# Turning the first batches' q and k with plain products in an attention and two-MLP kernel

## The chip, the cores and the metric

The kernel runs on one core of a Trainium2 chip. The metric is device time in microseconds (us) of one execution. Three timed runs of the kernel before gave 852.64, 853.40 and 854.97 us; the median is 853.4 us.

## The reference

Batched attention with a narrow causal mask feeds a SwiGLU layer and then a SoLU layer with a norm. All inputs are float32 or, for the weights, float64 words.

```python
def attn(q, k, v):                       # each 4 x 8 x 576 x 64
    scores = q @ k.T / sqrt(64)
    # heads 0-3: the 32 last keys; heads 4-7: every 4th of the 128 last keys
    scores = where(mask, scores, -1e9)
    return softmax(scores) @ v

x = attn(q, k, v).transpose(0, 2, 1, 3).reshape(2304, 512)
x = (silu(x @ w_gate) * (x @ w_val)) @ w_out         # 512 -> 1536 -> 512
h = x @ w_in                                         # 512 -> 1024
s = h * softmax(h)
out = ((s - mean(s)) / sqrt(var(s) + 1e-6) * g_ln) @ w_out2
```

## The kernel before

**Stages.** The 2304 tokens are cut into 12 blocks of 192. Per block, stage A is the gate and value products (line 1458), B the product with w_out (line 1542); per 128 tokens, C is the product with w_in (line 1590) and D the last one (line 1718). These run on TensorE (PE) as three float16 passes each, since every operand is split into a high and a low float16 part. The weights come as float64 words in 1 MB loads (line 667); VectorE (DVE), ScalarE (ACT) and GpSimd (POOL) turn the words into float32 and split them (lines 690 to 870), one half slab after the other.

**Attention of batches 0 and 1.** These two batches (FIRST = 2) work in float32 and in pairs of heads, four pairs a batch. `load_qk` brings q or k of a pair into one tile: head 0 on partitions 0 to 47, head 1 on partitions 64 to 111, twelve rows of 64 numbers on each partition. `prep_T` then turns the tile on TensorE: twelve steps, in each one 48x64 piece of each head against a 48x48 identity, the piece being the loaded weights and the identity what streams. Head 0's piece goes through TensorE's transpose form (line 1130, one instruction), head 1's is an ordinary float32 product (line 1132, which the chip runs as two instructions, called passes below). Both heads write one PSUM bank pair, head 0 on PSUM partitions 0 to 63, head 1 on 64 to 127. ACT or DVE copies the result out (lines 1145, 1148). With q and k, four pairs and two batches there are 16 turned tiles, 192 steps. Behind them `g1` makes scores (lines 1306 and 1313), `g2` turns the probabilities (line 1358) and `g3` multiplies by v (line 1392). Batches 2 and 3 turn q and k by DMA and are not touched.

**What sets the order.** Nothing is left to a scheduler on the chip. At build time every piece of work is a step with an engine, a cost and its dependences; the class `Plan` plays the engines through with these costs and takes, of the steps that are ready first, the one with the lowest number in the table `PRI` (2190 numbers). The instructions stand in each engine's queue in that order. Where the plan finds TensorE idle before its 320th us, it puts in products of `ones` with itself (line 379, 128 columns each, "fills" below). The plan's cost of one turned tile is 12 x `ttc` = 12 x 0.09 = 1.08 us at full clock; `ttc` is the same before and after. SP issues nearly all loads in the plan's order, and a load waits in that queue for its buffer.

Of the kernel before, what the change touches and what calls it, by code (L numbers as in the profile page):

```python
# [334 lines left out]
def kernel(  # L335
# [13 lines left out]
    nc = tc.nc  # L349
# [173 lines left out]
    def dve(n):  # L523
        return n / 960 + 0.065
# [4 lines left out]
    def act(n):  # L529
        return n / 1200 + 0.09  # L530
# [1524 lines left out]
```

## Time and profile before

| | before |
|---|---|
| timed runs, median (range) | 853.4 us (852.64 to 854.97) |
| the profiled execution, its own time | 854.95 us |
| its span, first to last instruction | 852.8 us |
| PE busy | 838.3 us (98%) |
| DVE, ACT, POOL busy | 492.2 (58%), 438.0 (51%), 214.6 us (25%) |
| mean granted TensorE clock | 0.928 of full speed |

Busy is the time in which an engine had an instruction in hand; for PE it is no measure of how fast that work went. The granted clock is 1.0 at 2.4 GHz and 0.5 at 1.2 GHz. The profiled execution took 2.15 us more than its span and 1.55 us more than the median of the runs.

### The profile page before, as it was taken

What the parts mean: (1) busy time and instruction counts of PE and PEld (TensorE: products, weight loads), DVE (VectorE), ACT (ScalarE), POOL (GpSimd) and SP (SyncE); (2) the same over time, 40 slices, a digit from 0 to 9 for tenths busy, and PEclk for the clock granted to TensorE, in tenths of its full rate; (3) what the DMA queues carried; (4) which work ended last, traced back from release to release, by engine and by line L of the source; (5) the groups of instructions that cost most, each with busy time, mean ns of one, the idle gap of its engine ahead of it and who ended that gap; (6) DMA issues with size and microseconds to landing.
All of it is one profiled execution on the core that took longest, in us unless ns stands there. A gap on an engine that the chain in (4) does not pass through costs nothing.

```text
span 852.8 us, 21072 instructions
## 1 busy us (share of the span) xinstructions
PE 838.3 (98%) x8965; PEld 686.7 (81%) x8965; DVE 492.2 (58%) x1082; ACT 438.0 (51%) x825; POOL 214.6 (25%) x190
## 2 busy tenths in 40 slices
PE   9999999999999999999999999999999999999997
PEld 8777887978998897886778659888987789888753
DVE  1331852924988885976676777747738433132472
ACT  1123742843764366786877645666564443262432
POOL 2110410313265543222421423333432000020000
PEclk7665985966999999999999999999999999999999
DMA  9922234432413736114486254443311112001101
GB/s 226 280 96 69 69 116 126 136 103 73 128 51 91 184 115 144 51 40 92 86 161 121 60 95 106 86 90 80 69 37 33 32 29 42 14 1 26 39 0 50
DMA packets 132605, 73.46 MB, mean 86 GB/s; under 512 B 115104, under 2 KB 117280, under 8 KB 132000
## 3 DMA queue, kind: packets, MB, share of 16 engines
q1 hardware_dynamic: 132512, 72.12, 35.3%
q8 instruction: 70, 1.15, 0.6%
q14 instruction: 23, 0.19, 0.1%
HBM read 47.71 MB, written 4.72 MB: 61 GB/s over the span
## 4 chain that ended last, share of the span: by engine, by line
PE 91%; DVE 4%; SPq 2%; DMA 1%; ACT 1%; issue 1%; POOL 0%; ACTq 0%; POOLq 0%
PE ps L1458 33%; PE ps L1542 14%; PE ps L1590 10%; PE ps L1718 10%; PE ps L1132 7%; PE ps L1130 4%; PE ps L379 4%; PE ps L1392 2%; PE ps L1313 1%; PE ps L1199 1%; PE ps L967 1%; SPq L929 1%; PE ps L1265 1%; DMA vbig<-in_v_dram 1%; DVE area L603 1%
## 5 line engine op out<-in xcount | busy, mean ns | idle before, releaser
L1458 PE MATMUL ps<-x,gv 128*128 128x192 f16 x3456 | 307.7, 251 | 1.3 <-ACT ps L575 0.8
L1458 PEld LDWEIGHTS <-gv 128*128 128x128 f16 x3456 | 295.2, 100 | 9.8 <-issue 1.4
L1542 PE MATMUL ps<-uhl,area 128*128 128x192 f16 x1728 | 151.6, 247 | 1.5 <-DVE yhl L603 1.3
L1542 PEld LDWEIGHTS <-area 128*128 128x128 f16 x1728 | 143.3, 98 | 6.3 <-issue 2.0
L1590 PE MATMUL ps<-area,yhl 128*128 128x512 f16 x432 | 98.6, 379 | 0.0
L1718 PE MATMUL ps<-area 128*128 128x512 f16 x408 | 94.2, 379 | 0.8 <-DVE yhl L603 0.8
L1590 PEld LDWEIGHTS <-yhl 128*128 128x128 f16 x432 | 41.0, 98 | 44.6
L1470 ACT ACTIVATE si<-ps,c_gv 128x384 f32<-128x384 f32 x72 | 41.5, 578 | 64.1 <-PE ps L1458 63.4
L1479 DVE SCALAR_TENSOR_TENSOR u<-ps,c_gv,si 128x384 f32<-128x384 f32 x60 | 36.5, 610 | 63.4 <-ACT si L1470 63.4
L1718 PEld LDWEIGHTS <-area 128*128 128x128 f16 x408 | 38.9, 98 | 42.3 <-issue 1.1
L683 POOL TENSOR_TENSOR area<-area 128x512 int32<-128x512 int32 x28 | 40.6, 1466 | 78.9 <-DVE wsc L791 33.8
L1650 POOL TENSOR_TENSOR sml<-sml,nhalf 128x2 f32<-128x2 f32 x18 | 14.6, 809 | 156.1 <-DVE sml L1647 151.6
L1132 PE MATMUL ps<-ident,qk 48*64 48x48 f32 x264 | 51.1, 284 | 0.0
L1229 POOL TENSOR_TENSOR se<-se,sml 96x768 f32<-96x768 f32 x16 | 24.1, 1509 | 94.7 <-ACT si L1485 60.4
L1485 ACT ACTIVATE si<-u 128x384 f32<-128x384 f32 x60 | 31.1, 518 | 25.7 <-DVE u L1479 25.7
L1216 ACT ACTIVATE se<-se,sml 96x128 f32<-96x128 f32 x96 | 37.2, 388 | 7.2 <-DVE sml L1510 3.6
L1132 PEld LDWEIGHTS ps<-ident,qk 48*64 48x64 f32 x264 | 31.9, 170 | 9.6
L379 PE MATMUL ps<-ones 128*128 128x128 bf16 x462 | 37.0, 250 | 2.2 <-POOL kT L1095 1.5
L615 POOL TENSOR_TENSOR uhl<-u,uhl 128x768 f16<-128x768 f32 x12 | 19.7, 1668 | 75.5 <-ACT uhl L598 75.5
L379 PEld LDWEIGHTS <-ones 128*128 128x128 bf16 x462 | 33.8, 115 | 3.5 <-POOL kT L1095 1.5
L615 POOL TENSOR_TENSOR qk<-qk,qk 96x768 f16<-96x768 f32 x16 | 26.7, 1667 | 36.2 <-DVE qk L594 14.1
L1130 PE MATMUL ps<-ident,qk 48*64 48x48 f32 x132 | 34.1, 259 | 0.0
(249 smaller groups left out, 1235.2 us busy)
## 6 DMA issues: line engine op xcount, KB each, us to landing
area<-in_moe_w_out_dram SPq DMA_DIRECT2D x10, 1024.0 KB, 5.0
area<-in_moe_w_gate_dram SPq DMA_DIRECT2D x6, 1024.0 KB, 7.3
area<-in_moe_w_val_dram SPq DMA_DIRECT2D x6, 1024.0 KB, 8.5
area<-in_moe_w_in_dram SPq DMA_DIRECT2D x4, 1024.0 KB, 5.0
qk<-in_v_dram SPq DMA_DIRECT2D x9, 384.0 KB, 4.0
qk<-in_q_dram SPq DMA_DIRECT2D x20, 144.0 KB, 3.2
qk<-in_k_dram SPq DMA_DIRECT2D x18, 144.0 KB, 3.3
out_dram<-area SPq DMA_DIRECT2D x10, 256.0 KB, 2.0
```

What stands on the lines that cost most here:

```text
L379: nc.tensor.matmul(out=ps_t[4][:, 0, 256:384], lhsT=ones, rhs=ones, start=True, stop=True)
L615: step("POOL", n / 480 + 0.05, lambda: nc.gpsimd.tensor_tensor(out=lo(), in0=src(), in1=hi(), op=ALU.subtract), r=list(sk) + list(hk), w=lk)
L683: step("POOL", 1.27, lambda: nc.gpsimd.tensor_tensor(out=ti[:, x], in0=ti[:, x], in1=part[:, x], op=ALU.add), r=rk, w=tk)
L1130: nc.tensor.transpose(out=o, in_=i, identity=ident[rows, rows])
L1132: nc.tensor.matmul(out=o, lhsT=i, rhs=ident[rows, rows], start=True, stop=True)
L1216: nc.scalar.activation(out=smv[:, n], in_=smv[:, n], func=ACTF.Exp, bias=nm[:, n:n + 1], scale=1.0, accum_out=su[:, n:n + 1])
L1458: nc.tensor.matmul(out=cut(view()[:, ff, w]), lhsT=wt[:, a, kk, (f % 4) * 128:(f % 4) * 128 + 128], rhs=tokens(x[:, c, kk]), start=(w == 0 ...
L1470: step("ACT", act(384) + 0.06, lambda: nc.scalar.activation(out=si, in_=view()[:, :, 0], func=ACTF.Silu, scale=c_gv[:, b, 2 * ci:2 * ci + 1]),
L1479: nc.vector.scalar_tensor_tensor(out=uu, in0=view()[:, :, 1], scalar=c_gv[:, b, 2 * ci + 1:2 * ci + 2], in1=si, op0=ALU.mult, op1=ALU.mult)
L1542: nc.tensor.matmul(out=bk.get()[:, 0, cc * BLK:cc * BLK + BLK], lhsT=whl[6 + f // 4][:, a, f % 4, c * 128:(c + 1) * 128], rhs=uhl[:, e, f] ...
L1590: nc.tensor.matmul(out=bk.get()[:, half], lhsT=yhl[:, i, c, o:o + 128], rhs=w_in_hl[m][:, e, c % 2, half * 512:half * 512 + 512], start=(c ...
L1718: nc.tensor.matmul(out=bk.get()[:, 0], lhsT=zt[:, c, kk], rhs=whl[11 + half][:, e, kk % 4], start=(kk == 0 and n == 0), stop=(kk == 7 and ...
```

## The change

In `prep_T` both heads' pieces are ordinary products with the identity; the branch with the transpose form is gone. Costs in the plan change: a pair's q or k load 0.78 to 1.0, v loads 2.9 to 3.6 and 2.7 to 2.6, copying a turned tile out +0.2 on DVE and +0.25 on ACT. `PRI` is another table, so that the steps of all engines stand in another order. No step is added or taken away. The count of fills, which the plan puts in by itself, goes from 462 to 646.

```diff
 PRI = [
-    4, 0, 1, 8, 3, 10, 31, 11, 13, 67, 33, 21, 18, 20, 62, 43, 36, 46, 122, 87, 71, 104, 197, 12,
...
+    2, 4, 3, 11, 6, 9, 7, 12, 16, 23, 43, 26, 22, 41, 67, 73, 80, 97, 35, 45, 55, 110, 149, 13,
...
             if b < FIRST:
-                load(0.78, [(t[64 * h:64 * h + QH], src[b, 2 * pr + h].rearrange("(p e) d -> p (e d)", p=QH)) for h in range(2)],
+                load(1.0, [(t[64 * h:64 * h + QH], src[b, 2 * pr + h].rearrange("(p e) d -> p (e d)", p=QH)) for h in range(2)],
                      key)
...
-        load(2.9 if pr < 2 else 2.7, fns, key, act=b == 0 and OPT["vact"][O0.index(pr)])
+        load(3.6 if pr < 2 else 2.6, fns, key, act=b == 0 and OPT["vact"][O0.index(pr)])
...
                     i, o = t[rows, D * e:D * e + D], view()[64 * h:64 * h + 64, e, 0:QH]
-                    if h == 0:
-                        nc.tensor.transpose(out=o, in_=i, identity=ident[rows, rows])
-                    else:
-                        nc.tensor.matmul(out=o, lhsT=i, rhs=ident[rows, rows], start=True, stop=True)
+                    nc.tensor.matmul(out=o, lhsT=i, rhs=ident[rows, rows], start=True, stop=True)
...
         if (OPT["qkc"][b] >> (2 * pr + n)) & 1:
-            step("DVE", dve(S), copy, r=[bk], w=dk)
+            step("DVE", dve(S) + 0.2, copy, r=[bk], w=dk)
         else:
-            step("ACT", act(S) + 0.05, hi, r=[bk], w=dk)
+            step("ACT", act(S) + 0.3, hi, r=[bk], w=dk)
```

Three lines fall away in `prep_T`, so every line behind it has a number lower by 3 (line 1458 becomes 1455).

On PE, the first turned tiles stand behind the first products of v (line 967) and a row of fills. Before, the tile `qk` with q of pair 3, alternating:

```order
94 L379 MATMUL ps_65<-ones 128x128
95 L379 LDWEIGHTS ones
96 L379 MATMUL ps_65<-ones 128x128
97 L967 MATMUL ps_64<-yhl 128x128 x8
98 L1130 MATMUL ps_61<-ident,qk_89 64x48
99 L1132 MATMUL ps_61<-ident,qk_89 64x48
100 L1130 MATMUL ps_61<-ident,qk_89 64x48
101 L1132 MATMUL ps_61<-ident,qk_89 64x48
```

After, k of the same pair (the tile `uhl`) and its q, 24 equal products each:

```order
94 L379 MATMUL ps_65<-ones 128x128
95 L967 MATMUL ps_64<-yhl 128x128 x8
96 L1129 MATMUL ps_61<-ident,uhl 64x48 x24
97 L1129 MATMUL ps_62<-ident,qk_89 64x48 x24
98 L379 LDWEIGHTS ones
```

The alternation is gone, a second tile is turned at once, and 80 fills stand behind the two, where 66 stood behind one.

On SP, the loads that come first, as a difference (`yhl` and `vbig` are v, `qk`, `uhl` and the small `area` loads q and k, the large `area` loads weights):

```order
 L910 DMA yhl<-in_v_dram 32x2x256
 L910 DMA yhl<-in_v_dram 64x2x256 x3
 L910 DMA yhl<-in_v_dram 48x2x256
+L910 DMA uhl<-in_k_dram 48x768 x2
 L910 DMA qk_89<-in_q_dram 48x768 x2
 L667 DMA area<-in_moe_w_gate_dram 128x4x256
```

```order
 L910 DMA qk_90<-in_q_dram 48x768 x2
+L910 DMA area<-in_q_dram 48x768 x2
+L667 DMA area<-in_moe_w_val_dram 128x4x256
+L667 DMA area<-in_moe_w_gate_dram 128x4x256
 L910 DMA qk_91<-in_k_dram 48x768 x2
-L667 DMA area<-in_moe_w_val_dram 128x4x256
-L910 DMA uhl<-in_k_dram 48x768 x2
 L910 DMA area<-in_k_dram 48x768 x2
```

The k of pair 3 comes ahead of its q, and k of pair 2 (`qk_91`), the last load that the first scores need, now stands behind three weight loads in place of one.

On PE, where batch 0's first A products stand and batch 1's first turned tile is. Before, the tile came behind 36 of them:

```order
940 L1458 MATMUL ps_61<-x_97,gv_67 128x192
941 L1458 LDWEIGHTS gv_67
942 L1458 MATMUL ps_61<-x_97,gv_67 128x192
943 L1130 MATMUL ps_62<-ident,qk_89 64x48
944 L1132 MATMUL ps_62<-ident,qk_89 64x48
```

After, two of batch 1's tiles stand ahead of the first A product:

```order
907 L1129 MATMUL ps_63<-ident,qk_89 64x48 x24
908 L542 LDWEIGHTS ones
909 L542 MATMUL ps_65<-sml,ones 128x1
910 L1129 MATMUL ps_61<-ident,qk_90 64x48 x24
911 L1455 LDWEIGHTS gv_66
912 L1455 MATMUL ps_62<-x_97,gv_66 128x192
```

So stage A's start now waits in PE's queue for the first loads of batch 1's q and k.

## Rows read from the trace of the kernel before

**Rows 1.** The page: engines, then 40 slices: granted TensorE clock, GB/s of DMA.

```profile
PE 838.3 (98%) x8965; PEld 686.7 (81%) x8965; DVE 492.2 (58%) x1082; ACT 438.0 (51%) x825; POOL 214.6 (25%) x190
...
PEclk7665985966999999999999999999999999999999
...
GB/s 226 280 96 69 69 116 126 136 103 73 128 51 91 184 115 144 51 40 92 86 161 121 60 95 106 86 90 80 69 37 33 32 29 42 14 1 26 39 0 50
```

**Rows 2.** The chain that ended last, its shares of the span by line.

```profile
by line: PE ps L1458 32.6%; PE ps L1542 14.3%; PE ps L1590 10.3%; PE ps L1718 10.0%; PE ps L1132 7.4%; PE ps L1130 4.4%; PE ps L379 3.9%; PE ps L1392 1.9%; PE ps L1313 1.3%; PE ps L1199 1.2%; PE ps L967 1.0%; SPq L929 0.9%; PE ps L1265 0.8%
```

**Rows 3.** Groups by line and form: the transposes, busy us and mean ns.

```profile
L1130 PE MATMUL ps<-ident,qk 48*64 48x48 f32 x132 | 34.1, 259 | 0.0
...
L1130 PE MATMUL ps<-ident,uhl 48*64 48x48 f32 x36 | 9.6, 265 | 0.0
...
L1130 PE MATMUL ps<-ident,area 48*64 48x48 f32 x24 | 6.8, 283 | 0.0
```

**Rows 4.** Timeline of PE, first turned tile: start us, length us, line, tiles, count.

```profile
10.10 0.23 PE L1130 MATMUL ps<-ident,qk 48*64 48x48 f32 x1
10.26 0.31 PE L1132 MATMUL ps<-ident,qk 48*64 48x48 f32 x2
10.51 0.23 PE L1130 MATMUL ps<-ident,qk 48*64 48x48 f32 x1
...
11.04 0.28 PE L1130 MATMUL ps<-ident,qk 48*64 48x48 f32 x1
11.26 0.44 PE L1132 MATMUL ps<-ident,qk 48*64 48x48 f32 x2
11.63 0.28 PE L1130 MATMUL ps<-ident,qk 48*64 48x48 f32 x1
```

**Rows 5.** Busy time, granted clock and DMA by stretch of the span.

```profile
core 0: us, PE busy (x) PEld busy (x) DVE busy (x) ACT busy (x) POOL busy (x), PEclk, DMA share, GB/s
0.00:52.50 52.50, 50.99 (x351) 40.85 (x351) 10.14 (x20) 6.90 (x7) 7.99 (x24) 0.67 0.92 244
...
262.30:300.00 37.70, 36.00 (x606) 33.95 (x605) 31.49 (x70) 15.51 (x25) 22.50 (x19) 0.95 0.55 127
106.40:262.30 155.90, 155.26 (x1683) 136.11 (x1681) 97.34 (x200) 83.07 (x132) 42.41 (x36) 0.81 0.35 107
0.00:106.40 106.40, 104.40 (x1256) 83.24 (x1257) 39.03 (x105) 32.72 (x50) 22.02 (x41) 0.71 0.54 148
0.00:262.30 262.30, 259.65 (x2936) 219.35 (x2937) 136.37 (x304) 115.79 (x181) 64.42 (x76) 0.77 0.43 124
262.30:853.00 590.70, 578.66 (x6032) 467.35 (x6030) 355.79 (x779) 322.21 (x644) 150.13 (x115) 1.00 0.33 69
```

**Rows 6.** Timeline of PE at full clock: plain float32 products with v.

```profile
90.07 0.29 PE L1392 MATMUL ps<-se,yhl 48*64 48x16 f32 x4
90.21 0.27 PE L1392 MATMUL ps<-se,u 48*64 48x16 f32 x4
90.33 0.31 PE L1392 MATMUL ps<-se,yhl 64*64 64x32 f32 x6
...
103.36 1.95 PE L1392 MATMUL ps<-se,vbig 64*64 64x32 f32 x90
```

**Rows 7.** Timeline of PE at half clock: scores, four heads into one bank.

```profile
52.89 1.24 PE L1313 MATMUL ps<-kT,qT 64*32 64x64 f32 x40
54.06 0.45 PE L1306 MATMUL ps<-qx,id 32*128 32x320 bf16 x1
```

**Rows 8.** Timeline of PE at full clock: products of whole v tiles, float32.

```profile
21.61 2.03 PE L967 MATMUL ps<-vbig 128*128 128x128 f32 x16
23.57 0.23 PE L1130 MATMUL ps<-ident,qk 48*64 48x48 f32 x1
```

**Rows 9.** Timeline of PE at full clock: fills.

```profile
155.53 3.92 PE L379 MATMUL ps<-ones 128*128 128x128 bf16 x67
159.28 0.50 PE L1358 MATMUL ps<-ident,se 128*128 128x128 f32 x3
```

**Rows 10.** Pieces of the chain: the same 24 A products at either clock.

```profile
183.76 3.96 PE ps L1458 x24
...
212.78 1.98 PE ps L1458 x24
```

182 rows, old and new, of the table PRI are left out of this document.

## The prediction

> **What bounds the kernel now.** I read the page first: TensorE has something in hand for 98% of the span, and the row of granted clocks splits the span in two [rows 1]. Up to slice 12 (some 260 us) the clock is mostly between 0.5 and 0.9 of full speed; behind it, 0.9 and more. By stretches [rows 5]: from 0 to 262.3 us, which ends where stage B begins, PE is busy for 259.65 us at a mean clock of 0.77, while DVE is busy for 136.37, ACT for 115.79 and POOL for 64.42; from there on PE runs at 1.00. So in the first 262 us the other engines are half idle, and PE is slow, not short of time: the end of that stretch is set by how long PE's queue takes. Next I ask what fills the queue. In the chain of waits, lines 1132 and 1130, the turning of q and k of batches 0 and 1, hold 7.4% and 4.4% [rows 2]: 11.8% of 852.8 = 100.6 us, all of it in this stretch, for work that the plan counts at 16 x 1.08 = 17 us. The count is 132 + 36 + 24 = 192 transposes [rows 3], one in each step.
>
> The timeline shows one step at either clock [rows 4]. At full clock a transpose starts at 10.10, the two passes of the plain product at 10.26, the next transpose at 10.51: 0.41 us a step. At half clock it is 11.04 to 11.63, 0.59 us. With 192 steps in 100.6 us the mean is 0.524, so 63% of them ran at half clock (121 x 0.59 = 71.4 us, 71 x 0.41 = 29.1 us). Nothing in a step runs beside anything else: 0.16 us from transpose to product and 0.25 from product to transpose, though the two heads use different halves of TensorE's rows and columns.
>
> **The change part by part.**
>
> *The turned tiles.* 192 transposes go and 192 plain products, 384 passes, come. The trace has no such tile, so the price comes from plain float32 products alone. The nearest row has the same weights, 48x64, in two places side by side [rows 6]: 8 passes between 90.07 and 90.33, 0.033 us a pass. They stream 16 columns, q and k stream 48; but a few lines below, 32 columns and four places cost 1.95/90 = 0.022, so the streamed columns are not what counts there. A step has four passes: 0.13 us; a tile 12 x 0.13 = 1.56 us; 16 tiles 25.0 us. Lower end: 0.022 a pass, 16.7 us. Upper end: nothing overlaps and a pass costs what it costs in the mixed step, 0.125 us at full clock (0.25 for two) and 0.185 at half clock (0.37 for two) [rows 4]; a step is then 0.50 or 0.74 us. I take 0.13, since its weights and the two places are those of the new step. Saved: 100.6 - 25.0 = 75.6 us, all on the path.
>
> The Trainium skill speaks against the low price: "TensorEngine Tiling (Array Packing)", Gotcha 1, says that different row tiles can't access the same PSUM bank simultaneously, and both heads of a turned tile write one bank. The trace disagrees. The scores put four heads, two on each half of the rows, into one bank [rows 7]: 40 passes of 64 columns in 1.17 us at half clock, 0.029 each. One such pass alone is an estimate of 0.12 us, from passes of twice the columns at twice the clock (16 in 1.96 us [rows 8]). So four did run side by side in one bank. What the rule would give is rival C.
>
> *The clock.* A mean of 0.77 over 262.3 us is 0.23/0.5 x 262.3 = 120.7 us at half clock [rows 5]; 71.4 of it are turned tiles, 49.3 other work, stage A's first products above all (24 of them 3.96 us against 1.98 [rows 10]). The clock falls in the middle of the first tile shown [rows 4], and where plain products of the same smallness follow each other it stays up [rows 6]. I expect the tiles no longer to pull it down: 49.3/2 = 24.6 us less. If it stays as it is, this term is 0 (rival A).
>
> *Fills.* 646 - 462 = 184 more. At full clock 67 take 3.75 us [rows 9], 0.056 each: +10.3 us if all delay something; 0 if they only fill waits. I take all, since a fill stands in PE's queue whether it is needed or not.
>
> *Costs in the plan.* The dearer loads and copies change no instruction; they act through the order alone. The copies out of PSUM stay 16.
>
> *Sum of PE's queue.* 854.95 (the profiled execution; 1.55 over the median) - 75.6 - 24.6 + 10.3 = 765.1 us. The stretch to 262.3 becomes some 171 us.
>
> *What is late next.* The cover under which the other engines worked is then gone, and I weigh them in two parts [rows 5].
> Up to 106.4 us (stage A begins): PE's part shrinks by half of the tiles (-50.3 + 12.5), by clock (0.71: 61.7 us at half clock, 35.7 of it tiles, so -13) and grows by 115 fills (+6.4): 62.0 us. The loads moved 148 GB/s x 106.4 us = 15.7 MB, which at the 244 GB/s of the first 52.5 us take 64.5 us. Also k of pair 2 now stands behind two more weight loads on SP, 2 MB or 8 us at that rate, and PE's queue waits for it with scores and everything behind. +4 us (bounds 0 and 10).
> From 106.4 to 262.3: -50.3 + 12.5 for tiles, -11.8 for clock (0.81: 59.2 us, 35.7 of it tiles), +2.9 for 51 fills: 109.2 us, against 97.34 us of DVE work, mostly converting weights that stage A waits for. That would be 89%; the busiest long stretch shown has 84% (31.49 of 37.7). 97.34/0.84 = 115.9: +7 us. At 75% it is 129.8: +21. ACT (83.07) and POOL (42.41) have room. Two tiles of batch 1 now stand ahead of the first A products, so these wait for that q and k too; the plan put them there behind 17 fills, and I leave it inside these bounds.
> Behind 262.3 us neither work nor clock changes, and PE already waits little (578.66 of 590.70 busy): 0, bounds -5 and +10.
>
> Forecast: 765.1 + 4 + 7 = **776 us**. Low end: passes at 0.022 (-8) and no new waits (-11, of which I grant all but 2 together with the tail's -5): about 754. High end: DVE at 75% (+14), half of the 49.3 us stay cold (+12): 802, rounded up to 804.
>
> **The rivals.**
> A. The clock stays as it is. Then tiles cost 1.56 us at full and, by the 0.029 us pass with four in parallel [rows 7], 12 x 4 x 0.058 = 2.8 us with two; at 63% cold 16 tiles are 37.5 us; the fills cost 14; nothing comes back from the clock: 854.95 - 100.6 + 37.5 + 14 = 806, and DVE and DMA are hidden again. For it: PE will have gaps where it waits for weights. Against: 184 more fills stand in just these gaps. A mixture with a tail made worse by the new order lies at 804 to 830.
> B. DVE becomes the bound of the whole stage A. At 75% of 97.34 us and without help from the order: 765 + 4 + 21 = 790. Its place is the products' wait for split weights. It decides once DVE's share passes 84%. It lies in the range.
> C. Slower: the two heads' products don't overlap, since both write one bank. A step is 0.50 us at full and 0.74 at half clock; 192 at today's mix are 192 x (0.63 x 0.74 + 0.37 x 0.50) = 125 us: +24.5, and +12 for fills, no gain in clock: 891. It decides from a step of (100.6 - 10.3)/192 = 0.47 us upwards. Against it: [rows 6, 7]. The Trainium skill's rule on banks, above, would end here.
> D. The new order costs more than the tiles bring, with loads late everywhere: to eat 90 us, DVE would have to fall to 136.37/262 = 52% again, with PE idle. I see no row for that.
>
> **How the numbers follow.** Forecast with B inside: 0.84. Rival A and its mixtures, 804 to 850: 0.09. Under 754: 0.04. C and D, slower: 0.03. A measurement of this kernel can tell 0.3% (2.6 us) from no change; no case but a chance mixture of A and D lies within it: 0.01. So faster 0.96, same 0.01, slower 0.03. The range 754 to 804 leaves out 16 in 100.
>
> **What would show it.** Right: a turned tile of 24 products, 48 passes, in 1.4 to 2.2 us at full clock; passes of both heads starting a few ns apart; granted clock 0.9 and more up to the start of stage B, and that start at 165 to 195 us; DVE at 75 to 90% while stage A runs; the first new waits of PE named by q, k loads or by DVE's split weights. Wrong: tiles of 6 us or more (C); a clock of 0.8 or less in the first 170 us (A); PE idle for over 25 us ahead of stage B (B, D); more than 600 us from the start of stage B to the end.

## The result, and the profile after

The changed kernel takes 781.58 us (median of four runs, 779.91 to 782.71), the kernel before, run beside it, 853.5 us (852.64 to 854.97). The ratio is 0.9154, with a 95% interval of 0.9132 to 0.9177: 72 us less. The profiled execution of after took 780.86 us, of which the span is 778.9. Measured beside other kernels a second time, the same program took 779.68 us.

The page of after, its engines, its row of granted clocks and its DMA row, which answer to [rows 1]:

```profile
span 778.9 us, 21846 instructions
...
PE 758.8 (97%) x9341; PEld 637.8 (82%) x9341; DVE 491.3 (63%) x1082; ACT 438.6 (56%) x823; POOL 217.0 (28%) x190
...
PEclk9969999999999999999999999999999999999999
...
GB/s 201 258 276 123 241 143 190 178 2 69 139 130 174 75 56 62 99 95 138 145 56 84 91 110 83 82 68 44 76 31 29 42 14 29 1 42 1 42 0 55
```

PE is still the engine that has work all the time, and DVE, ACT and POOL are busy for what they were (DVE 492.2 and 491.3 us). What changed is PE's queue, 79.5 us shorter though it holds 376 matmul records more, and the clock: one slice of 40 is below 0.9, where there were eight.

The chain that ended last, its shares of the span by line, beside [rows 2]:

```profile
PE ps L1455 34%; PE ps L1539 19%; PE ps L1715 12%; PE ps L1587 12%; PE ps L379 4%; PE ps L1129 3%; PE ps L1389 2%; PE ps L1196 1%; PE ps L967 1%; PE ps L1310 1%; PE ps L1262 1%; PE ps L1355 1%; POOL uhl L615 0%; DVE area L727 0%; DVE area L713 0%
```

The turned tiles (line 1129) hold 3% where two lines held 11.8%; by starts of instructions in the trace they are 26.2 us of PE's time, against 100.0 before. Next, the timeline of PE in the first 54 us (start us, length us, line, tiles, count, and in brackets the idle time just before and what ended it):

```profile
3.67 5.19 PE L379 MATMUL ps<-ones 128*128 128x128 bf16 x47 [3.67 <-POOL ones L1754]
8.66 2.27 PE L967 MATMUL ps<-yhl 128*128 128x128 f32 x16
10.86 1.60 PE L1129 MATMUL ps<-ident,uhl 48*64 48x48 f32 x48
12.30 1.57 PE L1129 MATMUL ps<-ident,qk 48*64 48x48 f32 x48
13.80 4.64 PE L379 MATMUL ps<-ones 128*128 128x128 bf16 x80
...
32.57 0.53 PE L1310 MATMUL ps<-kT,qT 64*32 64x64 f32 x22
36.04 0.76 PE L1310 MATMUL ps<-kT,qT 64*32 64x64 f32 x18 [2.94 <-issue]
...
43.95 5.36 PE L1129 MATMUL ps<-ident,uhl 48*64 48x48 f32 x96
49.24 3.70 PE L379 MATMUL ps<-ones 128*128 128x128 bf16 x33
```

A tile of 48 passes starts at 10.86 and the next at 12.30: 1.44 us, 0.030 us a pass, two heads side by side. At half clock (43.95 to 49.24) two tiles take 5.29 us. And there is something that the trace of before has nowhere: at 33.1 us PE stops in the middle of a run of equal products, for 2.94 us, with "issue" as the reason, so it waits for no tensor. When it goes on, it is at half clock.

The windows of after by stage (columns as in [rows 5]; stage A's first product, line 1455, starts at 79.66 us, where before had 106.25, and stage B's first, line 1539, at 180.43, where before had 255.16):

```profile
0.00:79.66 79.66, 72.77 (x1563) 67.09 (x1563) 44.16 (x114) 37.43 (x57) 23.07 (x41) 0.89 0.77 219
79.66:180.43 100.77, 99.36 (x1599) 96.42 (x1597) 90.65 (x183) 82.25 (x125) 40.62 (x33) 1.00 0.45 139
0.00:180.43 180.43, 172.13 (x3158) 163.52 (x3159) 134.80 (x296) 119.68 (x181) 63.68 (x74) 0.95 0.59 174
180.43:779.00 598.57, 586.68 (x6184) 474.26 (x6183) 356.45 (x787) 318.92 (x643) 153.28 (x117) 1.00 0.34 70
```

The same stretches of before, cut at the same two products, were 106.2, 149.0 and 597.8 us long. So 26.5 us come from ahead of stage A, 48.2 from stage A, and nothing from behind (+0.8). Stage A now runs at a granted clock of 1.00, and in it DVE is busy for 90.65 of 100.77 us, 90%, without PE waiting much: the waits of PE, the longest of the whole span first (us in total, times, longest):

```profile
PE ps L379 <- POOL ones L1754: 3.7, 1, 3.7
PE ps L1310 <- issue: 2.9, 1, 2.9
PE ps L1539 <- DVE yhl L603: 2.1, 2, 1.3
PE ps L1539 <- POOL uhl L615: 1.8, 1, 1.8
```

None of the four lies in stage A; PE's gaps between 79.66 and 180.43 us sum to 1.4 us.

### The profile page after: what moved, and what is told of

Its sections match the earlier page's. It is cut to its first block, busy times and chain, and to the rows that moved or that the text cites. A ratio compares the mean times of both kernels' runs of the same rounds, so it can differ in the third digit from the quotient of the medians.

```text
span 778.9 us, 21846 instructions
## 1 busy us (share of the span) xinstructions
PE 758.8 (97%) x9341; PEld 637.8 (82%) x9341; DVE 491.3 (63%) x1082; ACT 438.6 (56%) x823; POOL 217.0 (28%) x190
## 4 chain that ended last, share of the span: by engine, by line
PE 92%; DVE 5%; POOL 1%; issue 1%; ACT 1%; POOLq 0%; ACTq 0%; DVEq 0%
PE ps L1455 34%; PE ps L1539 19%; PE ps L1715 12%; PE ps L1587 12%; PE ps L379 4%; PE ps L1129 3%; PE ps L1389 2%; PE ps L1196 1%; PE ps L967 1%; PE ps L1310 1%; PE ps L1262 1%; PE ps L1355 1%; POOL uhl L615 0%; DVE area L727 0%; DVE area L713 0%
## 5 line engine op out<-in xcount | busy, mean ns | idle before, releaser
L1455 PE MATMUL ps<-x,gv 128*128 128x192 f16 x3456 | 293.0, 246 | 0.1
L1455 PEld LDWEIGHTS <-gv 128*128 128x128 f16 x3456 | 284.8, 98 | 4.8 <-issue 0.2
L683 POOL TENSOR_TENSOR area<-area 128x512 int32<-128x512 int32 x28 | 38.0, 1373 | 72.0 <-DMA u<-in_v_dram 21.5
L379 PE MATMUL ps<-ones 128*128 128x128 bf16 x646 | 43.9, 231 | 5.5 <-POOL ones L1754 3.7
L379 PEld LDWEIGHTS <-ones 128*128 128x128 bf16 x646 | 40.8, 104 | 6.5 <-POOL ones L1754 3.7
L615 POOL TENSOR_TENSOR qk<-qk,qk 96x768 f16<-96x768 f32 x16 | 29.0, 1812 | 49.0 <-DVE qk L594 22.5
L598 ACT ACTIVATE yhl<-ps,rel 128x384 f16<-128x384 f32 x24 | 13.6, 578 | 40.1 <-PE ps L1539 35.8
L1612 ACT ACTIVATE area<-ps,sml 128x1024 f32<-128x1024 f32 x18 | 21.6, 1202 | 23.2 <-DVE sml L1607 14.6
L1667 ACT ACTIVATE area<-area,sml 128x1024 f32<-128x1024 f32 x17 | 21.0, 1236 | 21.9 <-DVE sml L1661 21.8
L603 DVE SCALAR_TENSOR_TENSOR yhl<-ps,rel,yhl 128x384 f16<-128x384 f32 x24 | 14.5, 611 | 27.4 <-ACT yhl L598 20.1
```

The source lines that it names most:

```text
L379: nc.tensor.matmul(out=ps_t[4][:, 0, 256:384], lhsT=ones, rhs=ones, start=True, stop=True)
L615: step("POOL", n / 480 + 0.05, lambda: nc.gpsimd.tensor_tensor(out=lo(), in0=src(), in1=hi(), op=ALU.subtract), r=list(sk) + list(hk), w=lk)
L683: step("POOL", 1.27, lambda: nc.gpsimd.tensor_tensor(out=ti[:, x], in0=ti[:, x], in1=part[:, x], op=ALU.add), r=rk, w=tk)
L1455: nc.tensor.matmul(out=cut(view()[:, ff, w]), lhsT=wt[:, a, kk, (f % 4) * 128:(f % 4) * 128 + 128], rhs=tokens(x[:, c, kk]), start=(w == 0 ...
```

## Experiments

Theory 1, which the prediction used: the change of form between transpose and product, 24 times a tile, is what cost before, and half clock came with it; the new order and its 184 fills only follow. Rivals: the new order itself brings a good part; a transpose is dear by itself; the heads' lying side by side doesn't matter; the fills cost their 10 us; DVE is what bounds stage A. In each run the ratio is to the kernel before on the same chip.

### Products alone, in the old order

The kernel before, with nothing changed but the form of the first head's pieces; its table, its costs and its 462 fills stay:

```diff
-                    if h == 0:
-                        nc.tensor.transpose(out=o, in_=i, identity=ident[rows, rows])
-                    else:
-                        nc.tensor.matmul(out=o, lhsT=i, rhs=ident[rows, rows], start=True, stop=True)
+                    nc.tensor.matmul(out=o, lhsT=i, rhs=ident[rows, rows], start=True, stop=True)
```

> The kernel before with plain products for both heads, all else (table of order, costs, 462 fills) as before. Theory (the turned tiles and the clock they pull down made the difference, the new order adds little): a tile takes 1.4 to 1.6 us at full clock, the first 260 us shrink by 80 to 100 us, and the time is 770 to 800 us. Rival (the new order and the earlier loads made it): the saved PE time comes back as waits for loads and split weights in the old order, 815 us or more.

Measured: 775.01 us (770.77 to 778.41), ratio 0.9103 [0.9064, 0.9142]. Five lines give the whole gain and a little more. The windows of this kernel, to the first product of A, to the first of B, and on:

```profile
0.00:71.60 71.60, 64.65 (x1350) 57.99 (x1351) 38.42 (x105) 32.42 (x49) 21.52 (x40) 0.86 0.82 219
71.60:171.80 100.20, 100.11 (x1649) 96.69 (x1647) 91.14 (x175) 80.48 (x128) 41.02 (x34) 1.00 0.49 157
171.80:768.00 596.20, 583.46 (x6162) 471.81 (x6161) 365.54 (x804) 325.82 (x651) 154.50 (x118) 1.00 0.33 71
```

Against the windows of after: 213 matmuls fewer stand ahead of stage A (two turned tiles and over a hundred fills), A starts 8 us earlier in this execution, the fastest of its four (770.77 us), and it lasts as long as in after with 50 matmuls more in it. The new order moved work ahead of A and got nothing back in A.

It was run again, beside after itself and beside the old order with fills of double width:

> Plain products in the old order once more, beside the changed kernel. Theory (the new order brings nothing of its own): 773 to 778 us, 3 to 9 us under the changed kernel. Rival (the first set's 775 was chance): 779 to 784.

> The changed kernel as it is, for the comparison with the other runs of this set: 779 to 783 us, a gap of PE of 2 to 3 us in the first scores near 33 us with half clock behind it.

> Plain products in the old order, and every two fills made one of 256 columns, 231 fewer products in PE's queue. Theory (the gap of 3.6 us at 41.7 us, where a 16 KB block of instructions came late, hangs on how many instructions stand ahead): the gap moves or goes; 768 to 774 us if it goes, 775 to 778 if it falls on another place under full DMA load. Rival (PE waited for data there): gap in the same turned tile.

Measured on one chip: the old order 772.5 us (772.15 to 778.61), ratio 0.9071 [0.9047, 0.9095]; after 779.68 (776.87 to 783.25), 0.9145 [0.912, 0.9171]; the old order with wide fills 776.23 (772.74 to 778.28), 0.9091 [0.9069, 0.9113]. The intervals of the first two don't overlap: the old order is ahead by some 5 to 7 us and has the lowest median here. The wide fills add nothing to it that can be told apart. Their longest stop (the section on the hardware has more on these) is in score products, 3.79 us, and not in the turned tile of the old order's first run; but in the old order's second run it is in score products as well, so the move proves nothing about the fills. Which part of the new order costs those microseconds is not settled: the profiled execution of this second run was its slowest (778.61 us), with stage A starting at 79.1 us after 34 us at half clock, so it doesn't show the lead that the median has.

### Transposes in the new order

After, with the two forms put back:

```diff
-                    nc.tensor.matmul(out=o, lhsT=i, rhs=ident[rows, rows], start=True, stop=True)
+                    if h == 0:
+                        nc.tensor.transpose(out=o, in_=i, identity=ident[rows, rows])
+                    else:
+                        nc.tensor.matmul(out=o, lhsT=i, rhs=ident[rows, rows], start=True, stop=True)
```

> The changed kernel with the transpose form put back for head 0; new order, costs and 646 fills stay. Theory: tiles cost 100 us again where they now cost 26, the clock falls in them again, and the fills add; 860 to 885 us, slower than the kernel before by the 184 fills and by loads that it doesn't need so early. Rival (the new order alone is worth much): 820 us or less.

Measured: 864.14 us (863.24 to 865.64), ratio 1.0137 [1.0107, 1.0167]. The tiles take 96.8 us again, some 106 us ahead of stage B are at half clock again, and the new order with its 184 more fills makes the kernel slower by 12 us. How much of the 12 are the fills is not shown: no run has this order, transposes and the old fills. With the run above this settles that the gain is the tiles' and not the order's.

### Transposes and products, each in a row

The kernel before, with only the two loops exchanged: the 12 transposes of one head, then the 12 products of the other.

```diff
-            for e in range(12):
-                for h in range(2):
+            for h in range(2):
+                for e in range(12):
```

> The kernel before with the steps of a tile in another order: the 12 transposes of head 0 first, then the 12 products of head 1. Work and table of order as before. Theory (what costs is the change between the two forms, twice in each of the 192 steps): one change a tile is left; 12 transposes at 0.05 to 0.1 us and 24 passes at 0.058 us are 2.0 to 2.8 us a tile at full clock in place of 4.9, and the time is 780 to 815 us. Rival (a transpose is itself slow, 0.15 us or more wherever it stands): a tile stays at 4 us or more at full clock, 835 us or more.

Measured: 784.31 us (784.03 to 784.59), ratio 0.9199 [0.9159, 0.9238]. One tile at full clock in its timeline (line 1130 the transposes, 1132 the products):

```profile
17.84 0.70 PE L1130 MATMUL ps<-ident,qk 48*64 48x48 f32 x12
18.47 1.59 PE L1132 MATMUL ps<-ident,qk 48*64 48x48 f32 x24
20.00 0.70 PE L1130 MATMUL ps<-ident,qk 48*64 48x48 f32 x12
```

Twelve transposes take 0.63 us, 0.053 each; twelve products, 24 passes, 1.53. A transpose is the cheaper form when others of its kind stand beside it. With 24 changes of form a tile took 12 x 0.41 = 4.9 us at full clock [rows 4]; with two it takes 2.16 (16 tiles: 40.2 us with those at half clock). So the change of form is what was paid: the same transposes without it bring 68 us, and products in the same old order 77. The Trainium skill, "TensorEngine Tiling (Array Packing)", Key Properties, says that changing the tiling mode drains TensorE. The shapes of the two forms are the same here, so the rule doesn't name this case; the rows show what it would look like: nothing of one form runs beside the other.

The clock went back up too: in this kernel the stretch of stage A, with transposed tiles in it, is granted 1.00, where before had 0.81 with the same ones [rows 5]. Ahead of stage A it is granted 0.80, against 0.71: some 31 us there are still at half clock.

```profile
0.00:77.60 77.60, 72.56 (x1255) 65.29 (x1256) 38.56 (x105) 32.47 (x49) 21.56 (x40) 0.80 0.75 202
77.60:182.70 105.10, 105.05 (x1553) 101.12 (x1551) 91.28 (x175) 80.31 (x128) 40.49 (x34) 1.00 0.47 149
```

### One head after the other, all products

After, with the same exchange of loops, so that no two neighbours use different halves of the array.

```diff
-            for e in range(12):
-                for h in range(2):
+            for h in range(2):
+                for e in range(12):
```

> The changed kernel with the products of a tile in another order: the 12 of head 0 first, then the 12 of head 1, so that neighbours lie in the same place of TensorE. Theory (the low price comes from two heads side by side): 48 passes at 0.058 us are 2.8 us a tile at full clock in place of 1.44; 16 tiles cost some 20 us more of PE's queue, of which waits and fills hide a part: 785 to 803 us. Rival (side by side plays no part, each pass costs 0.03 us anyhow): tile 1.4 us and 780 to 784 us.

Measured: 806.58 us (804.91 to 808.26), ratio 0.946 [0.9414, 0.9507]: 25 us more than after, somewhat above what was expected. Two rows of its timeline, the first 45 passes of one tile and those of the next:

```profile
11.11 2.63 PE L1129 MATMUL ps<-ident,uhl 48*64 48x48 f32 x45
...
13.73 2.64 PE L1129 MATMUL ps<-ident,qk 48*64 48x48 f32 x45
```

A tile takes 2.6 us at full clock against 1.44, and all 16, with those at half clock, 49.2 against 26.2: 23 of the 25 us. Alternating the heads is worth nearly a factor of two, though both write the same bank. This decides the question of the bank that the prediction raised, against the Trainium skill's "TensorEngine Tiling (Array Packing)", Gotcha 1, as far as two heads in two halves of a bank's partitions go. The clock is at half for 41 us ahead of stage B here, where after has 17, and first falls at 16.1 us, in the second of its tiles: it falls also where all tiles are of one form.

### The fills

Without any of them, and with each pair made into one of 256 columns:

```diff
     def idle(n):
-        for _ in range(n):
-            nc.tensor.matmul(out=ps_t[4][:, 0, 256:384], lhsT=ones, rhs=ones, start=True, stop=True)
+        return
```

```diff
-        for _ in range(n):
+        for _ in range(n // 2):
+            nc.tensor.matmul(
+                out=ps_t[4][:, 0, 256:512].rearrange("p (a f) -> p a f", a=2), lhsT=ones,
+                rhs=ones.unsqueeze(1).to_broadcast([128, 2, 128]), start=True, stop=True)
+        for _ in range(n % 2):
```

> The changed kernel without any fills. Theory of the prediction (each of the 646 delays PE by 0.056 us): 36 us less in the queue, minus what the clock takes back. If fills only stand where PE would wait anyway and hold the clock up: PE is idle in their place, granted clock in the first 180 us falls to 0.6 to 0.8, and the time rises to 790 to 830 us. If they do delay: 750 to 775 us.

> The changed kernel with every two fills of 128 columns made one of 256: the same columns, 323 products and as many weight loads fewer in PE's queue. Theory (PE stood still for 2.9 us at 33 us because a 16 KB block of its instructions came late behind full DMA queues, and the clock fell to half for 17 us): block borders move, the gap at 33 us with its 17 us of half clock goes or moves to a place with less traffic; 771 to 778 us if it goes. Rival (PE waited for data at this place): the gap stays in the middle of the same scores, and the time within 1 us of the changed kernel.

Measured: without fills 779.66 us (778.76 to 781.83), ratio 0.9151 [0.9125, 0.9177], the same as with them; with wide ones 778.37 (774.98 to 781.82), 0.9132 [0.9094, 0.917], not told apart from after either. Both things that were expected of the run without fills are missed: neither did their time come back, nor did the kernel get slower. Without fills PE is busy for 23.7 us less; behind its first instruction it idles for 13.0 us ahead of stage A and 11.5 in it, and has 41 us at half clock up to stage B (after, counted alike: 3.2, 1.4 and 17.1). The page's engines and clock, PE's waits, and the stretch of stage A:

```profile
PE 735.1 (94%) x8695; PEld 612.8 (79%) x8695; DVE 493.0 (63%) x1082; ACT 437.9 (56%) x823; POOL 216.4 (28%) x190
...
PEclk9785889999999999999999999999999999999999
```

```profile
PE ps L966 <- DMA yhl<-in_v_dram: 5.9, 1, 5.9
PE ps L541 <- DVE wsc L791: 4.2, 1, 4.2
PE ps L1454 <- DVE x L1475: 3.5, 1, 3.5
PE ps L1128 <- DMA qk<-in_k_dram: 3.4, 1, 3.4
```

```profile
79.70:181.80 102.10, 90.62 (x1384) 87.02 (x1383) 90.19 (x182) 81.25 (x124) 41.08 (x33) 0.96 0.43 136
```

The fills hide waits for DVE and for loads that are there in any case, and what they cost they give back in clock. In stage A PE is now busy for 90.62 us and DVE for 90.19, and the stretch is 102.1 us against 100.8: neither engine alone fills it.

### The ones ahead of everything

The first fill of after waits until 3.67 us for the tile of ones, which POOL writes behind other steps. Here it is written ahead of the plan:

```diff
-        step("POOL", 0.1, lambda: nc.gpsimd.memset(ones, 1.0), w=[("ones",)])
+        step("POOL", 0.1, lambda: None, w=[("ones",)])
...
+        nc.gpsimd.memset(ones, 1.0)
         P.emit()
```

> The changed kernel with the tile of ones, which the first fills wait for until 3.67 us, set first on GpSimd. Theory (PE's queue is the bound from its start): the first fill starts at 1.3 to 1.6 us and the time falls by 1 to 2.3 us, to 779 to 780.5. Rival (the first loads of v and k, not PE, set when the first tiles are turned): the first turned tile starts at 10.9 us as before, and the time stays within 0.7 us.

Measured: 777.14 us (776.64 to 780.69), ratio 0.9115 [0.9089, 0.914], not told apart from after. That lies under the range of the theory and under that of the rival, and the profiled execution is the slowest of its five (780.69 us). In it PE starts 2.7 us earlier, the first turned tile 2.9 earlier (7.94 us, so the rival fell), and stage A starts at 79.4 us, 0.2 earlier. Its timeline shows where the rest went:

```profile
0.99 4.86 PE L379 MATMUL ps<-ones 128*128 128x128 bf16 x47 [0.99 <-POOL ones L2021]
...
17.25 2.02 PE L967 MATMUL ps<-vbig 128*128 128x128 f32 x16 [0.85 <-DMA vbig<-in_v_dram]
...
23.63 0.32 PE L1129 MATMUL ps<-ident,area 48*64 48x48 f32 x3 [1.49 <-issue]
...
35.86 0.62 PE L1310 MATMUL ps<-kT,qT 64*32 64x64 f32 x18 [2.08 <-issue]
```

PE arrives earlier at the v that isn't there yet, and stops three times by "issue" (a stop of 0.72 us at 14.6 us isn't in the rows) where the first run of after stopped once; the second run of after has three such stops as well.

### More and less work on DVE

In the conversions of eleven of the twelve half slabs of w_gate and w_val, the last instruction (it merges the weights' sign) twice, and in another kernel not at all. The second leaves that sign out of those weights.

```diff
-            step("DVE", dve(1024), lambda: nc.vector.scalar_tensor_tensor(
-                out=ti, in0=hi, scalar=-0x40000000, in1=ti, op0=ALU.bitwise_and, op1=ALU.bitwise_or), r=rk, w=tk, port=True)
+            def last():
+                for _ in range(2 if n < 6 else 1):
+                    nc.vector.scalar_tensor_tensor(
+                        out=ti, in0=hi, scalar=-0x40000000, in1=ti, op0=ALU.bitwise_and, op1=ALU.bitwise_or)
+
+            step("DVE", dve(1024), last, r=rk, w=tk, port=True)
```

The other has `range(0 if n < 6 else 1)`, and both have the same at the other place where the sign is merged.

> The changed kernel with one more DVE instruction (the last of a conversion once more, 1.2 us, to the same values) in 10 of the 12 half slabs of w_gate and w_val: some 12 us more work on DVE up to the end of stage A's first three blocks, where DVE is busy for 90.65 of 100.8 us. Theory (DVE still has room, PE is the bound): half or less comes through, 782 to 788 us. Rival B of the prediction (DVE is the bound of stage A): all of it, 791 to 795 us.

> The changed kernel without 11 DVE instructions of 1.2 us: the last one of each conversion (the sign of the weight) is left out for the half slabs of w_gate and w_val that have it. 13 us less DVE work up to stage B. Theory (DVE bounds stage A from both sides, since 14 us came through when the same were added): 768 to 774 us. Rival (PE's queue with its fills is as long as DVE's work, so that less of DVE frees nothing): 778 us or more.

Measured: more 795.76 us (793.11 to 799.11), ratio 0.9338 [0.93, 0.9376]; less 779.41 (774.67 to 780.48), 0.9127 [0.9104, 0.9151]. Stage A's stretch in the one with more and the one with less, and what PE waits for longest in the first:

```profile
81.70:193.60 111.90, 103.52 (x1599) 99.94 (x1598) 98.51 (x187) 80.77 (x123) 41.67 (x33) 0.96 0.40 123
```

```profile
80.41:180.69 100.28, 99.38 (x1601) 96.44 (x1598) 80.82 (x175) 81.85 (x125) 40.67 (x33) 1.00 0.44 140
```

```profile
PE ps L379 <- DVE wsc L553: 4.8, 1, 4.8
```

With 15.0 us more on DVE ahead of stage B (149.8 against 134.8), B starts 13.2 us later: nearly all of it comes through, and PE idles for 8.4 us in stage A. With 12.9 us less (122.0), nothing comes back: DVE's share falls from 90% to 81%, and PE, busy for 99.38 of 100.28 us, holds the stretch as it was. That DVE bounds stage A is right in the one direction alone, and the forecast that less work there would be faster fell. The two are balanced: either of them, made longer, is the bound, and no run here made both shorter. Of PE's 99.38 us a part are fills; the kernel with less on DVE and no fills wasn't run.

## Why the prediction was right or wrong

The time, 780.86 us for the profiled execution, lies 5 us above the forecast of 776 and within the range. Of the signs that it named one failed: the first new waits of PE are for the ones and by "issue", not for q, k or split weights. Step by step:

- **The turned tiles.** Right: 26.2 us for 16, forecast 25.0, and 0.030 us a pass at full clock where 0.033 was taken from the row with the same weights. Two of the tiles at half clock make the rest. The choice of that row, and not of the cheaper one with four places, is what made the term good; that the heads must lie side by side for it was shown by exchanging the loops.
- **The clock.** Right in mechanism: 17.1 us at half clock up to the start of stage B, where before had 119.5. Most of it came with the alternation: the grouped transposes have 30.7 us, all ahead of stage A. All of the 17.1 us come behind PE's stop at 33.1 us, which the forecast didn't have; that stretch costs 8.5 us.
- **The fills.** Wrong in its assumption. "I take all" counted 10.3 us; taking all of them out changed nothing (779.66 us). They stand in PE's queue, but where they stand PE would wait.
- **Ahead of stage A.** Mis-sized: 62 us of queue and 4 of waits, 66 in all; measured 79.66. Four things make it longer: the ones (3.67 us, where before had its first fill at 1.51), the stop of 2.94 us, 8.5 us of half clock behind it, and two tiles of batch 1, 3.1 us, which the sum left in stage A though the order shown puts them ahead. What the forecast did name, 4 us for k of pair 2 behind two more weight loads, is not among PE's waits. Together this is 12.7 of the missing 13.7 us. The sum had no term for an engine that waits for nothing in the program; the trace of before has one such stop, of 0.17 us, and no row showed it.
- **Stage A.** Mis-sized the other way. It was counted at 109.2 us of PE's queue and 7 of waiting for DVE, 116 in all, from marks that end at 262.3 us, where the prediction has stage B begin; its first product is at 255.16 us, so that the sum is 7 us less, some 109, and measured were 100.77. Of the 8.3 us, 3.1 are the two tiles that moved ahead; the rest is the wait for DVE. DVE was thought unable to go beyond the busiest stretch shown, 84%; it ran at 90%, and at 91% in the old order, with PE idle for 1.4 us and 0.1 us. The step that failed took a share that DVE happened to have, in a stage where nothing asked for more, as a limit.
- **Behind stage B's start.** Right: 598.57 us against 597.8 on equal marks.

The two mis-sized parts, +13.7 and -8.3 us, nearly cancel. So the total is better than its terms: it rests on the tiles and the clock, and these two were right.

Of the rivals, A (the clock stays) didn't come; what it would have been is seen in no run. B came only when DVE was given more work. What C feared, no overlap of the heads, was made by hand in the run with one head after the other: even so a tile took 2.6 us and not 6, and the time was 806.6. D, that the new order costs more than the tiles bring, is wrong in size, and right in its sign: with products in both, the new order with its fills costs 5 to 7 us, and with transposes in both 12. A reader of the diff who expected its large table to carry the gain would have been misled; it is the branch of four lines.

## What to carry to other kernels

Price a small TensorE operation by what stands beside it in the queue, not by its own length: the same transposes cost 4.9 us a tile in alternation with products, 2.16 in a row, and plain products of two heads in two halves of the array 1.44. An engine's busy share is a bound only where something waits for that engine; to learn how far it can go, give it more work and less work, and believe the direction that moves the time. When a change comes with a new order, try the change alone in the old order: here that kernel has the lowest median.

## What the runs showed of the hardware

**PE can wait for its own instructions.** In the stop at 33.1 us nothing in the program holds PE. Windows of after around it (columns as above), and the DMA queues' packets from 33 to 37 us (packets, MB, share of 16 engines):

```profile
30.00:33.00 3.00, 3.00 (x113) 2.50 (x109) 2.21 (x4) 2.17 (x2) 1.76 (x2) 1.00 0.96 352
33.00:36.00 3.00, 0.11 (x7) 0.00 (x0) 0.34 (x3) 0.00 (x0) 1.28 (x2) 1.00 1.11 221
36.00:40.00 4.00, 3.96 (x101) 2.97 (x102) 1.58 (x4) 0.66 (x2) 0.18 (x2) 0.51 1.23 193
```

```profile
q1 hardware_dynamic: 1397, 0.80, 111.5%
q8 instruction: 1, 0.02, 2.0%
```

The DMA engines are full (share 1.11), and one packet of the instruction queue, 16 KB, starts at 33.35 us and takes 1.30 us; the clock is 0.51 behind the stop. The other kernels with plain products in alternating heads have such stops too, the longest of each 1.2 (without fills) to 3.8 us (old order, wide fills). One of them comes at a fixed place of the program and not at a fixed time: in the second run of after, with the ones first, and with more or less work on DVE, PE stops ahead of the same 18 score products, to go on between 35.86 and 38.04 us. In PE's records that is instruction 1,218. With wide fills the stop is at instruction 1,217, which is no longer in the scores, but in products of v:

```profile
35.10 1.05 PE L971 MATMUL ps<-u 128*128 128x128 f32 x7
37.98 2.27 PE L971 MATMUL ps<-u 128*128 128x128 f32 x9 [1.83 <-issue]
```

But one program can stop at several places: the old order stops longest in a turned tile in its first run (to 45.35 us, 3.61 us of "issue"; the packet starts at 42.92) and in score products in its second (to 36.50 us, 3.02 us).

An estimate from the page: 1.39 MB in the two instruction queues for 21,846 instructions are 64 bytes each, so a packet is some 256 instructions. A tile of 96 instructions (a weight load and a pass, 48 times) takes 1.44 us, so a packet lasts 3.8 us at that rate; before, a step of three passes took 0.41 us, and a packet some 17.

The records of all fourteen traces bear this out. Counted in PE's weight loads and products (with its few semaphore instructions), queue q8 brings one packet for each 256: 73 for after's 18,731, 70 for before's 17,976. PE has 24 stops by "issue" in the fourteen, of 0.17 to 3.79 us. In that count each of the 24 stands 193 or 194 instructions beyond a multiple of 256, whatever the kernel and whatever the work there: every stop is at a border between two blocks of 256. And each ends 1.2 to 1.7 us after the end of the packet that has the border's number in the queue. Of the 955 borders without a stop, PE came to all but seven more than 1.7 us after their packet's end.

So these stops are waits of PE for the next block of its own instructions. In 23 of the 24 the other DMA traffic held a share of 0.94 or more in the 4 us before the packet started (the 24th is the one of 0.17 us, in before), and PE had needed 3.0 to 6.9 us for the block ahead. A block that is done fast and a loaded DMA go together there; no run changed one of the two alone, so how much each counts is not shown. What the stops cost in all runs stays open, and so does what the half clock behind them costs: with one head after the other there is no stop, and 41 us are at half clock.

**Fills are free here in both directions.** 646 of them, 43.9 us of PE's records on the page, change nothing that can be measured: up to stage B, behind PE's first instruction, there are 24.5 us of gaps and 41 us at half clock without them, 4.6 and 17.1 with them.

**The form matters more than the operation.** A float32 transpose of 48x48 in a row of its kind takes 0.053 us, a plain product of the same piece 0.064 a pass and two passes, alone in its half; only the change between them is dear.
